# One batch's scores in two feed-forward banks, and two batches' small products issued form by form

## The chip, the cores and the metric

The kernel runs on one core of one Trainium2 chip. The metric is the device time of that core in microseconds (us). In what follows PE is the matrix engine (PEld its weight loads), DVE the vector engine, ACT the scalar engine, POOL the general one, and SP the engine whose queue issues nearly all transfers. PSUM is the memory into which PE writes its sums; it has eight banks.

## The reference, cut to what matters

The first half is a recurrent attention ("RetNet") over 768 tokens, 4 batches and 8 heads of 64 dimensions. Its output, with the heads of a token side by side (3072 tokens of 512 features), goes through a feed-forward network with a leaky rectifier.

```python
for t in range(S):
    state = gamma[None, :, None, None] * state + np.einsum('bhd,bhe->bhde', k[:, :, t], v[:, :, t])
    y[:, :, t] = scale * np.einsum('bhd,bhde->bhe', q[:, :, t], state)
...
h = x @ w_in
g = np.maximum(0.01 * h, h)
return (g @ w_out).astype(np.float32)
```

All of q, k, v are float32 here; the two weight matrices arrive as float64, so the kernel itself turns their 64-bit words into float32.

## The kernel before, in words

The recurrence is worked in chunks of 128 tokens (`C`), six chunks (`c` = 0 to 5) for each of four batches (`b` = 0 to 3). For one chunk of one batch the steps are these:

- `score` or `score_apart` (both through `scores_to`, line 182): 32 products of the chunk's keys and queries, with 64 rows and 64 columns of the PE array in use ("64*64" in the profile). `score` takes one tile of the pool tag `att` (two tiles of two banks each); `score_apart` takes two tiles of the tag `ff` (four tiles of one bank each, otherwise used by the feed-forward).
- `masked` (line 204) or, a half at a time, `masked_apart` (line 348): DVE multiplies the scores with the causal mask, out of PSUM into a tile `am`.
- `reads` (line 219): 16 products of the state with the queries, 64*64, the first to write the batch's tile `yp` (tag `att`). After them POOL does a tiny memset (line 224) that stands as an ordering mark: `first_values` of the same batch waits for it.
- `last_values` (line 255): 16 products of values and masked scores for the last 64 tokens of the chunk, in a form with all 128 rows and 64 columns ("128*64").
- `first_values` (line 244): 16 such products for the first 64 tokens, 64*64.
- `state` (line 270): 16 products of keys and values, 128*64, into other columns of the same tile `yp`.
- `taken`: DVE scales the tokens out of `yp` into the feed-forward's input `x` (line 300), adds the new sums to the state (line 309) and decays it (line 313). With the second of these the `yp` tile is given back.
- `decay_v` on ACT (line 154, eight instructions) scales the batch's values ahead of the products that read them.

The feed-forward is cut into four units of hidden columns, and each 2-by-2 product of blocks is done with seven block products instead of eight (`seven`, line 585; `hidden` and `output` are its two layers). Only unit 0 of chunk 0 is done with plain products (`direct`, line 607, tiles `d`), a step at a time (`next(steps)`). All of these use the whole array, "128*128".

The weights' float64 words are turned into float32 a piece at a time: `next_powers` puts three instructions on ACT (lines 497, 501, 502), `next_mantissas` three on DVE (lines 511, 516, 523) and then issues the load of a later piece on SP's queue.

The order of the work is written out by hand: each engine executes its instructions in the order in which the program's lines issue them, and engines wait for each other's results and for tiles to come free. The change lies in the straight-line part for chunk 1, between `scored_later(0)` and the second call of `products_together`. In this stage PE's order is: a step of `direct`; scores of batch 0; a step of `direct`; scores of batch 1; the products of batches 0 and 1 (`products_in_turn(0)`); a step of `direct`; scores of batches 2 and 3; the first block product of the next unit (`A_h`); the products of batches 2 and 3 (`products_together(2)`); the last step of `direct`; and the other block products. DVE's order is: mask of batch 0; a mantissa round; mask of batch 1; a mantissa round; `taken` for batches 0 and 1; masks of batches 2 and 3; and so on.

Of the kernel before, what the change touches and what calls it, by code (L numbers as in the profile page):

```python
# [23 lines left out]
def kernel(  # L24
# [133 lines left out]
    def two_banks(name):  # L158
        return psum.tile([128, 2, HP, C], FP32, tag="att", bufs=2, name=name)

    def score(c, b):

        ps = two_banks(f"ap_{c}_{b}").rearrange("p j a t -> p j (a t)")[:, :, 0:NS]
        scores[c, b] = ps.rearrange("p j (m n t) -> p j m n t", n=3, t=C // 2)
        scores_to(heads[c, b][0], [scores[c, b][:, j] for j in range(2)])
# [8 lines left out]
    def scores_to(x, ps):  # L174
        for m in range(HP // 2):
            for i in range(2):
                for late in range(2):
                    for j in range(2):
                        s, a = i ^ j, 2 * m + i
                        to = (ps[j][ts(1 - s, 64), m, 1 + s] if late else  # L180
                              ps[j][ts(s, 64), m, 0 : 2 + s : 1 + s])
                        nc.tensor.matmul(to, lhsT=x[ts(j, 64), 1, a, ts(late, 64)],  # L182
                                         rhs=x[ts(j, 64), 0, a, late * 64 :])
# [3 lines left out]
    def new_am(c, b):  # L187

        i = turn[0]
        turn[0] = (i + 1) % (3 if (c, b) >= (2, 2) else 2)  # L190
        if i < 2:
            return work.tile([128, 2, HP // 2, 3, C // 2], FP32, tag=f"am{i}", name=f"am_{c}_{b}")
        place = new_t(1, f"am_{c}_{b}").rearrange("p i k n -> p (i k n)")[:, 0 : 2 * NS]
        return place.rearrange("p (j m n t) -> p j m n t", j=2, n=3, t=C // 2)
# [7 lines left out]
    def masked(c, b):  # L202
        am = new_am(c, b)
        nc.vector.tensor_tensor(
            out=am.rearrange("p j m n t -> p j m (n t)"),
            in0=scores[c, b].rearrange("p j m n t -> p j m (n t)"),
            in1=mask.rearrange("p n t -> p (n t)").unsqueeze(1).unsqueeze(1)
                .to_broadcast([128, 2, HP // 2, 3 * C // 2]), op=ALU.mult)
        scores[c, b] = am
# [5 lines left out]
    def reads(c, b):  # L215
        x = heads[c, b][0]
        ps = sums_at[c, b] = two_banks(f"yp_{c}_{b}")
        for j, m, i, a in pairs:
            mm = nc.tensor.matmul(ps[ts(i, 64), j, m, :], lhsT=st[b][ts(j, 64), a, :],  # L219
                                  rhs=x[ts(j, 64), 0, a, :], start=(m == 0), stop=False,  # L220
                                  skip_group_check=True)


        reads_done[c, b] = nc.gpsimd.memset(between, 0.0).ins
        tc.add_manual_dep(reads_done[c, b], mm.ins.name, IN_ORDER, reason="rows of the array")
# [5 lines left out]
    def values(c, b):  # L231
        if c == 0:
            sums_at[c, b] = two_banks(f"yp_{c}_{b}")
        last_values(c, b)
        first_values(c, b)

    def first_values(c, b):

        y, am, ps = heads[c, b][1], scores[c, b], sums_at[c, b]
        for m in range(HP // 2):  # L240
            for i in range(2):
                for j in range(2):
                    s, a = i ^ j, 2 * m + i
                    mm = nc.tensor.matmul(ps[ts(i, 64), j, m, 0:64],  # L244
                                          lhsT=y[ts(s, 64), 1, 2 * a + j, :],
                                          rhs=am[ts(s, 64), j, m, 0], start=False, stop=True,
                                          skip_group_check=True)
                    if (c, b) in reads_done:
                        tc.add_manual_dep(mm.ins, reads_done.pop((c, b)).name, IN_ORDER,
                                          reason="rows of the array")  # L250

    def last_values(c, b):
        y, am, ps = heads[c, b][1], scores[c, b], sums_at[c, b]
        for j, m, i, a in pairs:
            nc.tensor.matmul(ps[ts(i, 64), j, m, 64:], lhsT=y[:, 1, 2 * a + j, :],  # L255
                             rhs=am[:, j, m, 1 + (i ^ j)], start=(c == 0 and m == 0), stop=True,
                             skip_group_check=True)

    def for_state(ps):
        return ps[:, 0, HP // 2 :, :].rearrange("p a (two d) -> p (a two) d", two=2)  # L260

    def state(c, b):
        y = heads[c, b][1]
        sp = for_state(sums_at[c, b])
        for a in range(HP) if c < NC - 1 else ():
            sums_of(sp, y, a)

    def sums_of(sp, y, a, start=False):
        for j in range(2):
            nc.tensor.matmul(sp[ts(j, 64), a, :], lhsT=y[:, 0, 2 * a + j, :],  # L270
                             rhs=y[:, 1, 2 * a + j, :], start=start, stop=True,
                             skip_group_check=True)
# [65 lines left out]
    def score_apart(c, b):  # L338

        banks = [psum.tile([128, HP * C], FP32, tag="ff", bufs=4, name=f"ap{j}_{c}_{b}")[:, 0:NS]  # L340
                 for j in range(2)]
        scores[c, b] = [ps.rearrange("p (m n t) -> p m n t", n=3, t=C // 2) for ps in banks]
        scores_to(heads[c, b][0], scores[c, b])

    def masked_apart(c, b, j):
        if j == 0:
            weights_of[c, b] = new_am(c, b)
        nc.vector.tensor_tensor(
            out=weights_of[c, b][:, j].rearrange("p m n t -> p m (n t)"),
            in0=scores[c, b][j].rearrange("p m n t -> p m (n t)"),  # L350
            in1=mask.rearrange("p n t -> p (n t)").unsqueeze(1)
                .to_broadcast([128, HP // 2, 3 * C // 2]), op=ALU.mult)
        if j == 1:
            scores[c, b] = weights_of.pop((c, b))
# [96 lines left out]
    def next_powers(scratch=None, between=None):  # L451
        n = done["powers"]
        done["powers"] += 1
        if n < N_PIECES and f64:
            powers(n, scratch, between)
        elif between is not None:
            between()
# [18 lines left out]
    def next_mantissas():  # L476
        begin_mantissas()
        end_mantissas()
# [389 lines left out]
        score(1, b)  # L868
        masked(1, b)

    def products_in_turn(b):
        for i in range(2):
            reads(1, b + i)
            values(1, b + i)
        for i in range(2):
            state(1, b + i)

    def products_together(b):
        for f in (reads, last_values, state, first_values):
            for i in range(2):  # L880
                f(1, b + i)

# [5 lines left out]
    scored_later(0)  # L890
    decay_v(1, 1, nc.scalar)
    next(steps)
    score(1, 1)
    next_powers()
    next_mantissas()
    masked(1, 1)
    next_powers()
    products_in_turn(0)
    next_mantissas()
    decay_v(1, 2, nc.scalar)  # L900
    next_powers()
# [8 lines left out]
    last_sum(0)  # L910
    next_mantissas()
    products_together(2)
    next_powers()
    run(steps, {})
# [144 lines left out]
```

## Time and profile before

| | us |
|---|---|
| median of 4 runs (lowest, highest) | 658.36 (657.75, 658.77) |
| profiled execution, its own time | 658.36 |
| its span, from the first to the last instruction | 656.5 |
| PE busy in the span | 651.6 |
| DVE busy | 362.4 |
| ACT busy | 176.1 |
| PE busy in the stretch from 30.58 to 34.81 (products of chunk 1, batches 0 and 1) | 4.23 of 4.23 |
| PE busy in the stretch from 40.16 to 43.83 (products of chunk 1, batches 2 and 3) | 3.67 of 3.67 |

The profiled execution took as long as the median, 658.36 us, of which 1.8 us lie outside the span. The granted clock of PE was 1.00 over the whole span. A line of a timeline gives the start, the duration up to the end of the last instruction merged into it, the engine, the line of the kernel, the operation, output and input by tile names, the part of the array in use, the shape and the number of instructions. Consecutive products overlap on PE, so the cost of a group of products is read from its start to the start of the next group, not from its own duration.

### The profile page before, as it was taken

What the parts mean: (1) busy time and instruction counts of PE and PEld (TensorE: products, weight loads), DVE (VectorE), ACT (ScalarE), POOL (GpSimd) and SP (SyncE); (2) the same over time, 40 slices, a digit from 0 to 9 for tenths busy, and PEclk for the clock granted to TensorE, in tenths of its full rate; (3) what the DMA queues carried; (4) which work ended last, traced back from release to release, by engine and by line L of the source; (5) the groups of instructions that cost most, each with busy time, mean ns of one, the idle gap of its engine ahead of it and who ended that gap; (6) DMA issues with size and microseconds to landing.
All of it is one profiled execution on the core that took longest, in us unless ns stands there. A gap on an engine that the chain in (4) does not pass through costs nothing.

```text
span 656.5 us, 11361 instructions
## 1 busy us (share of the span) xinstructions
PE 651.6 (99%) x4937; PEld 568.9 (87%) x4937; DVE 362.4 (55%) x589; ACT 176.1 (27%) x323; POOL 22.2 (3%) x45
## 2 busy tenths in 40 slices
PE   8999999999999999999999999999999999999998
PEld 5888888888888888888888889888888888888887
DVE  5789969889887674243436414526423344431342
ACT  5854465264261002102102211300220210221210
POOL 1000000000000020001001001001000100000000
PEclk9999999999999999999999999999999999999999
DMA  9921312323322650030022004004001001000001
GB/s 336 405 98 33 128 65 85 108 65 97 128 69 83 245 185 0 1 127 3 1 96 98 1 1 129 1 17 178 0 1 52 14 1 49 17 0 1 1 0 65
DMA packets 15906, 49.00 MB, mean 75 GB/s; under 512 B 1768, under 2 KB 2152, under 8 KB 15856
## 3 DMA queue, kind: packets, MB, share of 16 engines
q1 hardware_dynamic: 15696, 47.72, 20.9%
q8 instruction: 39, 0.64, 0.4%
q10 hardware_dynamic: 160, 0.55, 0.2%
q14 instruction: 11, 0.09, 0.0%
HBM read 41.97 MB, written 6.29 MB: 74 GB/s over the span
## 4 chain that ended last, share of the span: by engine, by line
PE 98%; DMA 1%; DVE 0%; issue 0%; DVEq 0%
PE B_o L585 13%; PE A_o L585 13%; PE C_o L585 13%; PE A_h L585 12%; PE B_h L585 12%; PE C_h L585 12%; PE D_o L585 6%; PE D_h L585 6%; PE ap L182 2%; PE d L607 2%; PE yp L255 2%; PE yp L219 1%; PE yp L244 1%; PE sp L270 1%; DMA t<-decay_dram 1%; PE yp L270 0%
## 5 line engine op out<-in xcount | busy, mean ns | idle before, releaser
L585 PE MATMUL A_h<-x,w 128*128 128x256 f32 x368 | 87.7, 381 | 0.0
L585 PEld LDWEIGHTS A_h<-x,w 128*128 128x128 f32 x368 | 69.3, 190 | 9.6
L585 PE MATMUL A_o<-g,w 128*128 128x256 f32 x288 | 68.1, 379 | 0.0
L527 DVE TENSOR_TENSOR m<-m,B_h 128x512 f32<-128x512 f32 x23 | 15.8, 687 | 92.9 <-PE B_h L585 92.9
L585 PEld LDWEIGHTS A_o<-g,w 128*128 128x128 f32 x288 | 54.6, 190 | 7.5
L620 ACT ACTIVATE g<-g 128x512 f32<-128x512 f32 x69 | 42.0, 630 | 66.3 <-DVE g L527 66.3
L625 ACT COPY m<-A_h 128x512 f32<-128x512 f32 x23 | 13.5, 586 | 170.5 <-PE A_h L585 150.2
L527 DVE TENSOR_TENSOR m<-m,B_o 128x512 f32<-128x512 f32 x16 | 11.0, 685 | 64.4 <-PE B_o L585 64.4
L585 PE MATMUL B_h<-t,w 128*128 128x256 f32 x184 | 43.6, 380 | 0.0
L585 PE MATMUL B_h<-x,w 128*128 128x256 f32 x184 | 43.5, 379 | 0.0
L585 PE MATMUL C_h<-t,w 128*128 128x256 f32 x184 | 43.5, 379 | 0.0
L585 PE MATMUL D_h<-t,w 128*128 128x256 f32 x184 | 43.5, 379 | 0.0
L585 PE MATMUL C_h<-x,w 128*128 128x256 f32 x184 | 43.5, 379 | 0.0
L585 PEld LDWEIGHTS B_h<-t,w 128*128 128x128 f32 x184 | 34.8, 190 | 5.1 <-DVE t L530 0.4
L585 PEld LDWEIGHTS B_h<-x,w 128*128 128x128 f32 x184 | 35.0, 190 | 4.8
L585 PEld LDWEIGHTS C_h<-t,w 128*128 128x128 f32 x184 | 35.0, 190 | 4.8
L585 PEld LDWEIGHTS D_h<-t,w 128*128 128x128 f32 x184 | 35.0, 190 | 4.8
L585 PEld LDWEIGHTS C_h<-x,w 128*128 128x128 f32 x184 | 35.0, 190 | 4.8
L585 PE MATMUL C_o<-gd,w 128*128 128x256 f32 (+1 forms) x148 | 34.2, 373 | 0.0
L585 PE MATMUL C_o<-g,w 128*128 128x256 f32 (+1 forms) x148 | 34.2, 373 | 0.0
L530 DVE TENSOR_TENSOR gd<-g,gd 128x512 f32<-128x512 f32 x48 | 33.2, 692 | 1.7
L585 PE MATMUL B_o<-gd,w 128*128 128x256 f32 x144 | 34.1, 380 | 0.0
(131 smaller groups left out, 986.4 us busy)
## 6 DMA issues: line engine op xcount, KB each, us to landing
raw<-in_weights_dram SPq DMA_DIRECT2D x31, 512.0 KB, 4.0
kv<-in_kv_dram SPq DMA_DIRECT2D x17, 512.0 KB, 5.3
out_dram<-o SPq DMA_DIRECT2D x23, 256.0 KB, 2.1
qk<-in_qk_dram SPq DMA_DIRECT2D x10, 512.0 KB, 4.8
o<-in_qk_dram SPq DMA_DIRECT2D x8, 512.0 KB, 4.7
in<-in_qk_dram SPq DMA_DIRECT2D x5, 512.0 KB, 8.3
in<-in_kv_dram SPq DMA_DIRECT2D x3, 512.0 KB, 7.8
kv<-in_kv_dram SPq DMA_DIRECT2D x4, 256.0 KB, 7.4
```

Source lines behind the costliest of these rows:

```text
L182: nc.tensor.matmul(to, lhsT=x[ts(j, 64), 1, a, ts(late, 64)], rhs=x[ts(j, 64), 0, a, late * 64 :])
L219: mm = nc.tensor.matmul(ps[ts(i, 64), j, m, :], lhsT=st[b][ts(j, 64), a, :], rhs=x[ts(j, 64), 0, a, :], start=(m == 0), stop=False, skip_g ...
L244: mm = nc.tensor.matmul(ps[ts(i, 64), j, m, 0:64], lhsT=y[ts(s, 64), 1, 2 * a + j, :], rhs=am[ts(s, 64), j, m, 0], start=False, stop=True, ...
L255: nc.tensor.matmul(ps[ts(i, 64), j, m, 64:], lhsT=y[:, 1, 2 * a + j, :], rhs=am[:, j, m, 1 + (i ^ j)], start=(c == 0 and m == 0), stop=Tru ...
L270: nc.tensor.matmul(sp[ts(j, 64), a, :], lhsT=y[:, 0, 2 * a + j, :], rhs=y[:, 1, 2 * a + j, :], start=start, stop=True, skip_group_check=True)
L527: nc.vector.tensor_tensor(out=out, in0=a, in1=b, op=ALU.add)
L530: nc.vector.tensor_tensor(out=out, in0=a, in1=b, op=ALU.subtract)
L585: nc.tensor.matmul(to, lhsT=block(w, sa)[:, k, ts(i, 128)], rhs=rhs[:, k, a:z], start=(first and (i == 0 or split) and n == 0 and k == 0), ...
L607: nc.tensor.matmul(banks[r][:, i, :], lhsT=block(2 * u, r + 2 * kh)[:, k, ts(i, 128)], rhs=x[:, 2 * kh + th, k, :], start=(step == 0 and i ...
L620: nc.scalar.activation(g[:, i], g[:, i], AF.Prelu, alpha=0.01)
L625: nc.scalar.copy(out=got["m1"], in_=ps)
```

## The change

Three things change, all in chunk 1.

- The scores of batch 1 go into two tiles of the feed-forward's tag `ff`, one bank each, rather than into one tile of the tag `att`. The products themselves are the same 32.
- DVE therefore masks them in two instructions of 128x384 (`masked_apart`), rather than in one of 128x768, at the same place in its order.
- The products of batches 0 and 1 are issued together: the reads of both; then the last values and the state of each; then the first values of both. Before, each batch had its reads, last values and first values in turn, and the states of both came behind. The function serves batches 2 and 3 as well, and there only the order inside the middle changes: last values and state of batch 2 and then of batch 3, rather than the last values of both and then the states of both.

```diff
-    def products_in_turn(b):
+    def products_together(b):
         for i in range(2):
             reads(1, b + i)
-            values(1, b + i)
-        for i in range(2):
+        for i in range(2):
+            last_values(1, b + i)
             state(1, b + i)
-
-    def products_together(b):
-        for f in (reads, last_values, state, first_values):
-            for i in range(2):
-                f(1, b + i)
+        for i in range(2):
+            first_values(1, b + i)
...
     scored_later(0)
     decay_v(1, 1, nc.scalar)
     next(steps)
-    score(1, 1)
+    score_apart(1, 1)
     next_powers()
     next_mantissas()
-    masked(1, 1)
+    for j in range(2):
+        masked_apart(1, 1, j)
     next_powers()
-    products_in_turn(0)
+    products_together(0)
     next_mantissas()
```

The two functions that are called in place of `score` and `masked` were there already, for later chunks:

```python
def score_apart(c, b):
    banks = [psum.tile([128, HP * C], FP32, tag="ff", bufs=4, name=f"ap{j}_{c}_{b}")[:, 0:NS]
             for j in range(2)]
    scores[c, b] = [ps.rearrange("p (m n t) -> p m n t", n=3, t=C // 2) for ps in banks]
    scores_to(heads[c, b][0], scores[c, b])

def masked_apart(c, b, j):
    if j == 0:
        weights_of[c, b] = new_am(c, b)
    nc.vector.tensor_tensor(
        out=weights_of[c, b][:, j].rearrange("p m n t -> p m (n t)"),
        in0=scores[c, b][j].rearrange("p m n t -> p m (n t)"),
        in1=mask.rearrange("p n t -> p (n t)").unsqueeze(1)
            .to_broadcast([128, HP // 2, 3 * C // 2]), op=ALU.mult)
    if j == 1:
        scores[c, b] = weights_of.pop((c, b))
```

## The prediction, made before the changed kernel ran

> **What bounds the kernel.** I read the page first: busy time by engine, and the chain that ended last.
>
> ```profile
> PE 651.6 (99%) x4937; PEld 568.9 (87%) x4937; DVE 362.4 (55%) x589; ACT 176.1 (27%) x323; POOL 22.2 (3%) x45
> PE 98%; DMA 1%; DVE 0%; issue 0%; DVEq 0%
> ```
>
> The reader is to see that PE is the bound from end to end: 98% of the chain is PE's own instructions. So what the change is worth is the time that it takes out of PE's sequence, less any wait that it puts in. Next I read PE's timeline over the two stretches that hold chunk 1's small products, and one place in a later chunk where 32 reads lie between products of their own form.
>
> ```profile
> 30.58 0.62 PE L219 MATMUL yp<-in,states 64*64 64x128 f32 x16
> 31.13 0.69 PE L255 MATMUL yp<-am,in 128*64 128x64 f32 x16
> 31.75 0.46 PE L244 MATMUL yp<-am,in 64*64 64x64 f32 x16
> 32.12 0.67 PE L219 MATMUL yp<-in,states 64*64 64x128 f32 x16
> 32.72 0.69 PE L255 MATMUL yp<-am,in 128*64 128x64 f32 x16
> 33.34 0.46 PE L244 MATMUL yp<-am,in 64*64 64x64 f32 x16
> 33.73 1.15 PE L270 MATMUL yp<-in 128*64 128x64 f32 x32
> 34.81 1.99 PE L607 MATMUL d<-x,w 128*128 128x256 f32 x8
> ...
> 40.16 0.67 PE L219 MATMUL yp<-in,states 64*64 64x128 f32 x16
> ...
> 41.19 0.69 PE L255 MATMUL yp<-am,in 128*64 128x64 f32 x16
> ...
> 43.49 0.41 PE L244 MATMUL yp<-am,kv 64*64 64x64 f32 x16
> 43.83 1.99 PE L607 MATMUL d<-x,w 128*128 128x256 f32 x8
> ...
> 233.55 1.06 PE L219 MATMUL yp<-o,states 64*64 64x128 f32 x32
> 234.43 0.85 PE L182 MATMUL ap<-qk 64*64 64x128 f32 x32
> ```
>
> Read the starts. The 128 products of batches 0 and 1 take 34.81 - 30.58 = 4.23 us; the 128 products of the same kinds of batches 2 and 3, which the kernel issues kind by kind already, take 43.83 - 40.16 = 3.67. The array's form (64*64, 128*64) changes six times from the first read to `direct` in the first stretch (reads, last, first and reads, last, first, state, `direct`), three times in the second. Last I read DVE over the same stretch, since it decides when scores are masked and when banks come free.
>
> ```profile
> 31.12 0.95 DVE L204 TENSOR_TENSOR am<-ap,mask 128x768 f32<-128x768 f32 x1
> 31.98 0.42 DVE L511 TENSOR_SCALAR w<-raw 128x512 uint32<-128x512 uint32 x1
> ...
> 34.46 0.69 DVE L300 TENSOR_TENSOR x<-yp,dec 128x512 f32<-128x512 f32 x1 [0.54 <-PE yp L270]
> ...
> 36.45 0.41 DVE L309 TENSOR_TENSOR states<-states,yp 128x256 f32<-128x256 f32 x1
> 36.90 0.43 DVE L313 TENSOR_TENSOR states<-states,dec 128x256 f32<-128x256 f32 x1
> 37.71 1.82 DVE L204 TENSOR_TENSOR am<-ap,mask 128x768 f32<-128x768 f32 x2 [0.39 <-PE ap L182]
> ...
> 233.80 1.02 DVE L348 TENSOR_TENSOR am<-ap,mask 128x384 f32<-128x384 f32 x2
> ```
>
> The first line hides a wait of PE. The mask of batch 1 ends at 31.12 + 0.95 = 32.07, and the reads of batch 1 begin at 32.12, since their `yp` tile is the one that held batch 0's or batch 1's scores, two `att` tiles being all there are. The first values before them began at 31.75, and such a group takes 0.28 when the same kind follows (row 43.49 against the start of its neighbour, 43.21, in the same timeline), so the reads could have begun at 32.03: about 0.09 us of PE time was lost to the mask.
>
> **The products of batches 0 and 1, on the path.** What will they take when grouped? The reads now follow scores of their own form. Sixteen reads followed by the same form cost half of 234.43 - 233.55, so 0.44; sixteen followed by the change to 128*64 cost 31.13 - 30.58 = 0.55; together 0.99. From the first of the last values to `direct` the row is that of batches 2 and 3: 43.83 - 41.19 = 2.64. Sum 3.63, against 4.23: **-0.60 us**. The other bound takes the whole stretch of batches 2 and 3 as it stands, 3.67, whose reads follow a 128*128 product and pay for it: -0.56. I take -0.60, since reads behind scores is what the new order has.
>
> **Last values and state interleaved, both pairs.** Both are 128*64, 16 products each. In the second stretch the groups of these two kinds start at 41.19, 41.71, 42.17, 42.64 and the next form at 43.21: 0.47 for each group inside the row, whether the neighbour is of the same kind or the other. Order inside one form is costed at 0. For batches 2 and 3 that is all that changes, so 0 there.
>
> **Scores of batch 1 in `ff` banks.** The same 32 products, 0. They now wait for two `ff` tiles. In the built program these are the banks of `direct`'s first pair of tiles, which ACT emptied by 26.1 (two instructions of 0.6 from 24.92), while PE reaches these scores at 29.87: covered by 3.8 us. The same two banks pass on to the A and B tiles of the next block products, exactly as before, 6 us after the masks; every later `ff` tile has the bank that it had. The `att` tiles alternate with the halves exchanged, at no cost that I can name.
>
> **The mask in two instructions, off the path.** The row 233.80 shows two of 128x384 in 1.02 us, so the pair ends 0.07 later than the one of 0.95, at 32.14, and DVE's next instruction starts some 0.09 later (second mask at 0.475, twice, against 31.98 - 31.12 = 0.86). Who waits? PE's last values of batch 1, which come behind reads (0.99), last values (0.52) and state (0.47) from 30.58: at 32.56. Cover 0.42 us; if it were gone, PE would wait for the difference, with `direct` queued behind. [...]
>
> **DVE's chain behind it.** Its mantissa round now ends at 33.92 + 0.09 = 34.01. The tokens of batch 0 (L300) waited in the trace for the last product into that `yp` tile, the state's, until 34.46. In the new order the last product into it is batch 0's first values: they start at 31.57 + 2.02 = 33.59 (43.21 - 41.19 = 2.02), 16 of them end at about 34.05. So L300 starts about 34.05, 0.41 earlier than before. Then batch 1's state is added by 36.86 - 0.41 = 36.45, which is what the scores of batch 3 need for their tile; PE reaches these at 37.45 - 0.60 = 36.85. **Cover 0.40 us**, the smallest on this path. The mask of batch 2 is ready to go at 37.33 - 0.41 = 36.92 and its scores end at 37.11: it moves by the full 0.60, as do `A_h`, the products of batches 2 and 3 and all that follows them.
>
> **POOL and SP.** POOL's two marks follow the reads; the second now comes at about 31.6 instead of 32.94, and the first values that wait for it start at 33.87. Nothing else is queued on POOL. SP's order is unchanged; the weight load behind the moved mantissa round is issued 0.09 later and its reader on ACT is at 51.52, some 14 us after landing (4.0 us each).
>
> **Sum.** -0.60 against the profiled execution's own 658.36 us, which is the median too: **657.76 us**, 0.09% less. About 0.2% (1.3 us) is what a measurement of this kernel tells from no change, so the forecast is "same" with a small real gain inside.
>
> **Rivals.**
> 1. *Slower: DVE becomes the wait.* If DVE is late by more than 0.40 us at batch 1's state, PE waits in front of batch 3's scores; from 0.40 + 0.60 = 1.00 the kernel is slower than before. A whole mantissa round between the wrong steps (1.94, from 31.98 to 33.92) would give 658.36 - 0.60 + 1.94 - 0.40 = 659.3. For it: DVE is 84% busy in this stretch (3.56 of 4.23), and the tokens of batch 0 now hang on the end of a group that comes later in the order. Against it: the instruction that DVE then waits for is earlier in time than before, and the order on DVE is otherwise the same.
> 2. *Absorbed.* PE comes 0.60 earlier to something that doesn't move, a transfer or a conversion: 658.36. For it: the transfers are busy here (0.96 of their time from 30.58 to 34.81). Against it: in the list of waits none of PE's after 27 us is a transfer, and the conversions of this stage run behind PE's own results.
> 3. *More.* PE stalls at 57.88 us for DVE's emptying of the B bank (DVE L527 ends at 57.82); the eight products before it take 57.88 - 56.02 = 1.86 and its own 59.71 - 57.88 = 1.83, where such a group takes 1.73 in the steady rows: 0.23 in all. If a changed order freed that, 658.36 - 0.60 - 0.23 = 657.53. Against: DVE is busy without a pause from 43.74 to there and starts on PE's last product, so it shifts as PE does, and the bank is the same.
>
> **From the numbers to the chances.** The forecast case has 0.82, absorbed 0.08, slower by DVE 0.06, more 0.04. Runs of the kernel lie 0.61 below to 0.41 above their median. That puts the likeliest case within 657.15 to 658.17, and with the absorbed case and a little of its scatter the range is 657.1 to 658.5. Beyond 1.3 us on the fast side there is no mechanism (0.03 for scatter); on the slow side a part of rival 1 (0.04); the rest is within 0.2%.
>
> **What would show it.** After: reads of both batches in one run from 30.58 for about 0.99 us; the stretch to `direct` 3.6 us; `direct` at 34.2; the masks as two rows ending at 32.14; L300 at 34.05; all later rows 0.6 earlier, the stall at 57.3 still there. Wrong would be: a gap before the last values of batch 1 (mask late), a gap before the scores of batch 3 (bank late), or the 0.6 vanishing at a later wait.

## The result and the profile after

The changed kernel takes 657.30 us (median of 41 runs) against 658.39 us for the kernel before (61 runs, taken beside them). The medians differ by 1.09 us. The ratio on record, which is that of the means (657.45 to 658.36), is 0.9986, with a 95% interval of 0.9982 to 0.9991: 0.14% faster, or 0.92 us (0.59 to 1.19). That is "same" on record and inside the 0.2% of the forecast, but the interval lies wholly below 1, so the gain is real. Two later comparisons of the same two kernels, with 11 runs of the changed kernel each, gave 0.9990 (0.9981 to 0.9999) and 0.9989 (0.9980 to 0.9997).

The profiled execution of the changed kernel took 657.73 us, 0.43 above the median; it has a pause of PE ahead of the stretch in question, of which more below. The page's first and fourth parts read as before:

```profile
PE 650.8 (99%) x4937; PEld 568.3 (87%) x4937; DVE 361.5 (55%) x590; ACT 176.1 (27%) x323; POOL 22.3 (3%) x45
PE 98%; DMA 1%; DVE 0%; issue 0%; DVEq 0%
```

PE's timeline over the two stretches of small products, changed kernel (columns as before: start, duration, engine, line, operation, tiles, form, shape, count):

```profile
31.06 1.05 PE L219 MATMUL yp<-in,states 64*64 64x128 f32 x32
32.04 0.69 PE L255 MATMUL yp<-am,in 128*64 128x64 f32 x16
32.56 0.64 PE L270 MATMUL yp<-in 128*64 128x64 f32 x16
33.02 0.64 PE L255 MATMUL yp<-am,in 128*64 128x64 f32 x16
33.49 0.64 PE L270 MATMUL yp<-in 128*64 128x64 f32 x16
34.06 0.69 PE L244 MATMUL yp<-am,in 64*64 64x64 f32 x32
34.68 1.99 PE L607 MATMUL d<-x,w 128*128 128x256 f32 x8
36.61 0.90 PE L182 MATMUL ap<-in 64*64 64x128 f32 x32
37.33 0.85 PE L182 MATMUL ap<-qk 64*64 64x128 f32 x32
...
40.03 0.67 PE L219 MATMUL yp<-in,states 64*64 64x128 f32 x16
...
43.71 1.99 PE L607 MATMUL d<-x,w 128*128 128x256 f32 x8
```

The first stretch lasts 34.68 - 31.06 = 3.62 us where it lasted 4.23. The second, whose middle was reordered too, lasts 3.67 as before (3.674 from the unrounded starts of both kernels). DVE over the same time:

```profile
31.59 1.01 DVE L348 TENSOR_TENSOR am<-ap,mask 128x384 f32<-128x384 f32 x2
...
34.59 0.69 DVE L300 TENSOR_TENSOR x<-yp,dec 128x512 f32<-128x512 f32 x1
...
36.59 0.41 DVE L309 TENSOR_TENSOR states<-states,yp 128x256 f32<-128x256 f32 x1
```

The two masks end at 32.60, before the last values of batch 1 at 33.02. Batch 1's state is added by 37.00, before the scores of batch 3 at 37.33. No new wait stands in the stretch.

The traces allow a sharper comparison than the times. From the unrounded starts of the products I take three figures of each trace: the first stretch (first read of batch 0 to the plain products), the second (first read of batch 2 to the plain products), and the time from the end of the first stretch to the start of the kernel's last product. "Pause" means, here and below, that PE stands still although nothing that the profile shows holds it up.

| kernel | stretch 1 | stretch 2 | behind stretch 1 | ratio to the kernel before |
|---|---|---|---|---|
| before, three traces | 4.22, 4.22, 4.92 | 3.67 | 618.69, 618.20, 618.19 | 1 |
| changed, three traces | 3.63, 3.62, 3.63 | 3.67 | 618.19, 618.20, 618.20 | 0.9986, 0.9990, 0.9989 |
| scores apart alone | 4.08 | 3.67 | 618.20 | 0.9998 |
| grouping alone | 4.78 | 3.67 | 618.19 | 1.0009 |
| order by kind | 3.78 | 3.67 | 618.18 | 0.9991 |
| second pair in turn | 3.63 | 4.13 | 618.42 | 0.9993 |
| one more on DVE | 3.63 | 3.67 | 618.55 | 0.9996 |
| three more on DVE | 3.63 | 3.67 | 619.85 | 1.0014 |
| last sum later | 3.63 | 3.67 | 617.96 | 0.9985 |
| ACT late | 3.72 | 3.67 | 618.39 | 0.9993 |

Behind the stretch, the kernel before and the changed one agree to 0.01 us, save the first trace of before, which has one pause there. So what the change does to a trace it does inside the stretch, and all that follows comes as much earlier.

### The profile page after: what moved, and what is told of

Same layout as the page of the kernel before. It is cut to its first block, busy times and chain, and to the rows that moved or that the text cites. A ratio compares the mean times of both kernels' runs of the same rounds, so it can differ in the third digit from the quotient of the medians.

```text
span 655.9 us, 11361 instructions
## 1 busy us (share of the span) xinstructions
PE 650.8 (99%) x4937; PEld 568.3 (87%) x4937; DVE 361.5 (55%) x590; ACT 176.1 (27%) x323; POOL 22.3 (3%) x45
## 4 chain that ended last, share of the span: by engine, by line
PE 98%; DMA 1%; DVE 0%; issue 0%; DVEq 0%
PE B_o L585 13%; PE A_o L585 13%; PE C_o L585 13%; PE A_h L585 12%; PE B_h L585 12%; PE C_h L585 12%; PE D_o L585 6%; PE D_h L585 6%; PE ap L182 3%; PE d L607 2%; PE yp L255 2%; PE yp L219 1%; PE yp L244 1%; PE sp L270 1%; DMA qk<-in_qk_dram 1%; PE yp L270 0%
```

## The experiments

**Which half of the change brings the gain: scores apart alone.** The kernel before, with only the scores and the mask of batch 1 changed.

```diff
-    score(1, 1)
+    score_apart(1, 1)
...
-    masked(1, 1)
+    for j in range(2):
+        masked_apart(1, 1, j)
```

> The kernel before with batch 1's scores in two feed-forward banks and the mask in two halves, products still batch by batch. By the prediction's steps the reads of batch 1 no longer wait for the mask: 0.09 us less, the stretch 4.14 instead of 4.23, or 4.09 if the restart of 0.05 inside the reads goes too; total -0.1. Rival (the feed-forward banks themselves bring a gain or a wait): more than 0.3 either way.

PE's timeline of this kernel:

```profile
30.30 0.62 PE L219 MATMUL yp<-in,states 64*64 64x128 f32 x16
...
31.46 0.46 PE L244 MATMUL yp<-am,in 64*64 64x64 f32 x16
31.74 0.62 PE L219 MATMUL yp<-in,states 64*64 64x128 f32 x16
...
34.38 1.99 PE L607 MATMUL d<-x,w 128*128 128x256 f32 x8
```

The stretch is 4.08. The reads of batch 1 follow the first values of batch 0 after 0.28, where it was 0.37 (32.12 - 31.75) in the kernel before: the mask's wait is gone, and with it 0.05 of restart inside the reads, which took 32.72 - 32.12 = 0.60 behind the stop and 32.29 - 31.74 = 0.55 here. The wait's price in the first trace was thus 0.14 us. The ratio, 0.9998 (0.9989 to 1.0007), cannot tell 0.1 from nothing; the trace can.

**Grouping alone.** The changed kernel with `score(1, 1)` and `masked(1, 1)` put back.

```diff
-    score_apart(1, 1)
+    score(1, 1)
...
-    for j in range(2):
-        masked_apart(1, 1, j)
+    masked(1, 1)
```

> The changed kernel with batch 1's scores back in one tile of the attention banks and one mask, products still grouped. The reads of batch 1 then need the tile that the mask reads last, so PE waits after the reads of batch 0 until about 32.1 where it could go on at 31.0: the stretch 3.63 + 1.1 = 4.7 us, total +0.5 against the kernel before. Rival (the banks don't matter, grouping alone brings it all): the stretch 3.6, total -0.6.

```profile
30.83 0.62 PE L219 MATMUL yp<-in,states 64*64 64x128 f32 x16
32.37 0.67 PE L219 MATMUL yp<-in,states 64*64 64x128 f32 x16 [0.92 <-DVE am L204]
...
35.60 1.99 PE L607 MATMUL d<-x,w 128*128 128x256 f32 x8
```

PE stands after batch 0's reads until the mask (DVE L204) frees the tile: a step of 1.54 in place of 0.44. The stretch is 4.78 and the kernel slower than before, ratio 1.0009 (1.0001 to 1.0018), as forecast. Grouping without the second pair of banks loses; the scores in feed-forward banks are what lets it gain.

**The price of a change of form.** With the mask's wait out of the way, batch by batch costs 4.08 and grouped 3.63: 0.45 us for three changes of the array's form, 0.15 each. In the starts of these two traces the price stands where the form changes: the first product after a change comes 0.15 or 0.20 after the one before it, and where a new kind begins in the same form 0.04 or 0.05. Does it hold elsewhere? The changed kernel with the products of batches 2 and 3 issued in turn:

```diff
+    def products_in_turn(b):
+        for i in range(2):
+            reads(1, b + i)
+            values(1, b + i)
+        for i in range(2):
+            state(1, b + i)
...
-    products_together(2)
+    products_in_turn(2)
```

> The changed kernel with the products of batches 2 and 3 issued batch by batch, as those of 0 and 1 were before: three changes of the array's form more, and no mask to wait for. The measured price of three changes without the mask's wait is 4.08 - 3.63 = 0.45 us (scores apart alone against the changed kernel). Expected: that second stretch 3.67 + 0.45 = 4.12 us, total +0.45 against the changed kernel, so about 0.15 to 0.2 below the kernel before. Rival (the price was due to the place, the mask and the scores before it): less than 0.2.

```profile
39.76 0.67 PE L219 MATMUL yp<-in,states 64*64 64x128 f32 x16
...
43.89 1.99 PE L607 MATMUL d<-x,w 128*128 128x256 f32 x8
```

The second stretch takes 4.13: the price is that of the form, not of the place. But the kernel's trace is only 618.42 - 618.19 = 0.23 longer behind the first stretch, not 0.46. Half was given back later, and DVE's timeline shows why. It starts on batch 2's tokens when the products into batch 2's tile are done. In this order that is 0.34 us before the plain products begin:

```profile
43.55 1.29 DVE L300 TENSOR_TENSOR x<-yp,dec 128x512 f32<-128x512 f32 x2 [1.55 <-PE yp L270]
```

In the changed kernel it starts 0.10 before them, at 43.61 against 43.71:

```profile
43.61 1.29 DVE L300 TENSOR_TENSOR x<-yp,dec 128x512 f32<-128x512 f32 x2 [1.32 <-PE yp L244]
```

From there DVE waits for nothing for 14 us, up to the emptying of a bank for which PE waits (at 57.8). A DVE that starts earlier by PE's clock removes that wait of 0.23, and PE's groups there step by 1.72 and 1.73 with the second pair in turn:

```profile
56.09 1.89 PE L585 MATMUL A_o<-g,w 128*128 128x256 f32 x8
57.81 1.89 PE L585 MATMUL B_o<-gd,w 128*128 128x256 f32 x8
59.54 0.81 PE L585 MATMUL C_o<-gd,w 128*128 128x256 f32 x3
```

**That wait, tried directly.** The changed kernel with one DVE subtraction moved behind the emptying:

```diff
-                2: [next_powers], 3: [lambda: add_sums(1)]})
+                2: [next_powers], 3: [lambda: add_sums(1, last=False)],
+                4: [lambda: last_sum(1)]})
```

> The changed kernel with one DVE subtraction (the last of the four weight sums of unit 1, 0.61 us from start to start) moved behind the emptying of the B bank, which PE waits for at 57.8. In every trace but that of the second pair in turn, DVE works without a pause from 43.6 to there and PE loses 0.13 before the group and 0.10 in its first product. Expected: the emptying ends at about 57.1, before PE needs it at 57.6, and the 0.23 go: 617.96 us from the plain products to the last product instead of 618.19, total 0.23 below the changed kernel. Rival (PE waits there for something else): 618.19.

PE's timeline, the changed kernel first (three groups of eight products), then this one:

```profile
55.90 1.89 PE L585 MATMUL A_o<-g,w 128*128 128x256 f32 x8
57.75 1.99 PE L585 MATMUL B_o<-gd,w 128*128 128x256 f32 x8
59.58 0.59 PE L585 MATMUL C_o<-gd,w 128*128 128x256 f32 x2
```

```profile
55.52 1.89 PE L585 MATMUL A_o<-g,w 128*128 128x256 f32 x8
57.25 1.89 PE L585 MATMUL B_o<-gd,w 128*128 128x256 f32 x8
58.98 1.24 PE L585 MATMUL C_o<-gd,w 128*128 128x256 f32 x5
```

Steps of 1.85 and 1.83 become 1.73 and 1.73, and the time behind the stretch falls to 617.96. This version measured 657.14 us, ratio 0.9985 (0.9976 to 0.9994) to the kernel before; beside the changed kernel of the same chip, 657.36, it is the faster of the two by 0.22, which the times alone would not prove and the trace does.

**The order inside a form.** The changed kernel with last values of both batches, then states of both:

```diff
-        for i in range(2):
-            last_values(1, b + i)
-            state(1, b + i)
-        for i in range(2):
-            first_values(1, b + i)
+        for f in (last_values, state, first_values):
+            for i in range(2):
+                f(1, b + i)
```

> The changed kernel with the middle ordered as last values of both, then states of both. Inside one form the order costs nothing, but the last values of batch 1 come 0.47 us earlier and then begin 0.05 us before the second half of the mask is done: the stretch 3.63 to 3.7 us, total within 0.1 of the changed kernel. Rival (alternating last values and states costs or saves something itself): the stretch differs by over 0.2.

```profile
30.34 1.05 PE L219 MATMUL yp<-in,states 64*64 64x128 f32 x32
31.32 1.31 PE L255 MATMUL yp<-am,in 128*64 128x64 f32 x32
32.46 1.10 PE L270 MATMUL yp<-in 128*64 128x64 f32 x32
...
34.12 1.99 PE L607 MATMUL d<-x,w 128*128 128x256 f32 x8
```

DVE's two masks in the same trace:

```profile
30.99 1.02 DVE L348 TENSOR_TENSOR am<-ap,mask 128x384 f32<-128x384 f32 x2
```

The stretch is 3.78, more than the 3.63 to 3.7 expected. The 32 last values take 1.14 where 0.99 is their price (0.52 + 0.47): PE waited 0.10 for the mask's second half, which ended at 32.01, and restarted 0.05 slower. But the masks of this trace were themselves 0.12 late, starting 0.65 after the first read instead of 0.53. By these figures masks on time would have cost nothing (an estimate, with 0.02 to spare). The changed kernel's third trace has the same lateness (0.66) and a stretch of 3.63. For the second pair the two orders take the same 3.67. So the order itself is free, and what the state products between the last values buy is cover for the mask, 0.47 us of it; that is why the same lateness cost 0.15 in one order and nothing in the other.

**How thin is DVE's cover.** One, then three subtractions of 128x512 more on DVE, between the masks and the mantissa round; three shown:

```diff
     products_together(0)
+    for _ in range(3):
+        minus(parts[1][2][:, 0], x[:, 0], x[:, 0])
     next_mantissas()
```

> The changed kernel with one more 128x512 subtraction on DVE, between the masks and the mantissa round; its result is overwritten before it is used. It delays DVE by about 0.65 us. By the trace batch 1's state is added 0.33 us before the scores of batch 3 need its bank, and DVE waited 0.1 for batch 0's products: expected cost on PE 0.65 - 0.1 - 0.33 = 0.2 us, as a pause before the scores of batch 3. Rival (DVE's cover is larger, the next wait is elsewhere): 0.

> The same with three such subtractions: 1.9 us later on DVE, expected cost 1.9 - 0.43 = 1.5 us, split over a pause before the scores of batch 2 and one before those of batch 3, total about 0.8 us above the kernel before. Rival: under 0.5.

PE's timeline with one more, then with three:

```profile
36.47 0.90 PE L182 MATMUL ap<-in 64*64 64x128 f32 x32
37.33 0.90 PE L182 MATMUL ap<-qk 64*64 64x128 f32 x32
```

```profile
34.22 1.99 PE L607 MATMUL d<-x,w 128*128 128x256 f32 x8
37.08 0.90 PE L182 MATMUL ap<-in 64*64 64x128 f32 x32 [0.87 <-issue]
38.47 0.90 PE L182 MATMUL ap<-qk 64*64 64x128 f32 x32 [0.49 <-PE ap L182]
```

With one, the scores of batch 3 come 0.86 after those of batch 2 instead of 0.72: 0.14 lost there, 0.2 expected. (Of the rest of its 618.55, 0.05 lies inside these scores and 0.16 is a pause in a later chunk, at 344.23.) With three, both scores wait, 0.93 (2.86 from the plain products instead of 1.93) and 0.67, and the time behind the stretch is 1.66 longer, 1.5 expected; ratio 1.0014 (1.0005 to 1.0023). The added work delays DVE's mantissa round by 0.60 and by 2.05 us, and PE loses 0.19 and 1.65 around these scores. The place and the cover are as forecast: DVE may be 0.4 us late and no more.

**Is the gain more than 0.60?** The three ratios say 0.7 to 0.9 us, a little above what the first traces show. I had two ideas: pauses of PE that happen to be absent, or something systematic. Both kernels were traced again.

> The changed kernel once more, for a second trace. The trace of before has a pause of PE of 0.48 us at 344.58 us, in the middle of a group of state products that waits for nothing; the changed kernel's trace has one of 0.61 us at 23.55 instead. Theory A (only the products count: 0.60 us, the rest is the scatter of such pauses): the pauses sit elsewhere again in this trace, and the stretch from the first read of batch 0 to the plain products is 3.63 us. Theory B (the change also takes away a pause that the kernel before nearly always has): the changed kernel is again about 1.0 us below the kernel before, and this trace has no pause, so that its own time is about 657.2.

> The kernel before once more, for a second trace. So far every trace has the same 618.19 us from the plain products after the stretch to the last product, within 0.01, save the first trace of before, which has 618.69 with its pause of 0.48 at 344.58. Theory A (pauses come and go): no pause at 344.58 here, 618.2 us. Theory B (the kernel before nearly always pauses there): 618.7 us again. The stretch is 4.22 either way.

> The changed kernel a third time, on the same chip as the next one. Theory A: 3.63 us for the stretch, 618.19 us behind it, and the comparison with the kernel before -0.6 us, with pauses of 0.3 to 0.6 us that come and go in both. Theory B (the change also saves some 0.3 us outside the stretch): -0.9.

> The kernel before a third time: 4.22 us for the stretch and 618.19 behind it, 618.5 to 618.7 if it has the pause at 344.58 again, or another inside.

The pause at 344.58 in the first trace of before didn't come again in its other two. The pause near 23.55 is in two of the changed kernel's three traces and in none of before's, though up to there both programs are the same: pauses come and go, and theory B in the form that I gave it (before nearly always pauses there) fell. But the third trace of before showed something else, in the stretch itself:

```profile
31.47 0.46 PE L244 MATMUL yp<-am,in 64*64 64x64 f32 x16
32.54 0.67 PE L219 MATMUL yp<-in,states 64*64 64x128 f32 x16 [0.61 <-DVE am L204]
...
35.23 1.13 PE L607 MATMUL d<-x,w 128*128 128x256 f32 x4
```

Here the reads of batch 1 waited 0.8 us for the mask. ACT and DVE of the same trace tell why the mask was late:

```profile
23.52 2.02 ACT L154 ACTIVATE in<-in,dec 128x64 f32<-128x64 f32 x8 [2.71 <-DMA in<-in_kv_dram]
...
29.67 0.43 DVE L511 TENSOR_SCALAR w<-raw 128x512 uint32<-128x512 uint32 x1 [0.90 <-ACT z L501]
...
31.54 0.95 DVE L204 TENSOR_TENSOR am<-ap,mask 128x768 f32<-128x768 f32 x1
```

A transfer of values landed late, so ACT began its scaling at 23.52 (23.00 in the first trace, with PE's reads at 30.58 there and 30.30 here); DVE's mantissa round (L511) waited 0.90 for ACT instead of 0.20; and the mask, which stands behind that round, started 1.23 after the first read instead of 0.53. (In the changed kernel's second trace ACT began as late, at 23.57, but there PE itself paused for 0.57, up to 23.64, so that by PE's clock the mask was on time.) The last run tests what the changed kernel makes of the same lateness, with an ACT copy more ahead of ACT's part of the conversion:

```diff
     score_apart(1, 1)
+    nc.scalar.copy(out=parts[1][2][:, 0], in_=x[:, 0])
     next_powers()
```

> The changed kernel with one more 128x512 copy on ACT (about 0.6 us), ahead of the conversion steps that DVE's mantissa round waits for; its result is overwritten before use. It makes batch 1's mask late, as a late transfer did by 0.70 us in the third trace of before, where the reads waited and the stretch grew from 4.22 to 4.92. Theory C (the mask is at times late, the kernel before pays for all of it, the changed kernel has 0.4 us of cover): the mask starts about 1.2 us after the first read instead of 0.53, the stretch grows by only 0.2, to 3.8 us, a pause before the third of batch 1's last values, and the total is 0.2 to 0.3 above the changed kernel. Rival (the changed kernel pays as much): the stretch 4.2 to 4.3.

```profile
31.63 1.01 DVE L348 TENSOR_TENSOR am<-ap,mask 128x384 f32<-128x384 f32 x2
```

```profile
30.57 1.05 PE L219 MATMUL yp<-in,states 64*64 64x128 f32 x32
...
32.53 0.73 PE L255 MATMUL yp<-am,in 128*64 128x64 f32 x16
33.09 0.64 PE L270 MATMUL yp<-in 128*64 128x64 f32 x16
34.28 1.99 PE L607 MATMUL d<-x,w 128*128 128x256 f32 x8
```

The mask started 1.06 after the first read, 0.53 later than in an undisturbed trace, and the stretch grew by 0.09, to 3.72: the last values of batch 1 take 0.56 to the next group instead of 0.47, the wait being before the third pair of them, where the second half of the mask is first needed. The kernel before paid 0.70 for 0.70 of lateness; the changed one 0.09 for 0.53, so by an estimate from these two figures it would pay 0.26 for 0.70. That is a second gain, which a trace without the lateness doesn't contain. (Behind the stretch this run is 0.2 longer, 0.03 of it before the scores of batch 3 and most of the rest in a pause at 343.81.)

How much of the measured 0.7 to 0.9 us it makes up on average stays open: the mask was late by over 0.1 in one of three traces of before, by 0.12 or 0.13 in two of ten others, and the pauses scatter by as much as the difference.

## Why the prediction was right, and what it missed

*The sum.* The range (657.1 to 658.5) and the class ("same") held; 657.76 was forecast and 657.30 measured. The forecast gain of 0.60 lies only just inside the first comparison's interval (0.59 to 1.19), so the total is not as well explained as the main term. The main term, -0.60 for the products of batches 0 and 1, is what the traces show: 4.22 became 3.63, of which "scores apart alone" puts 0.14 down to the mask's wait, and the rest is the form's. The way of getting it, from rows of groups that already stood in the wanted order with the wanted neighbours, was good to 0.01. Its upper bound, the second stretch as it stands (-0.56), was 0.04 off: the first sixteen of those reads, which follow a 128*128 product, took 0.49 (40.03 to 40.52 in the changed kernel), and sixteen behind scores 0.44.

*The mis-sized term.* "About 0.09 us of PE time was lost to the mask" is the step that came out too small. In the first trace it was 0.14 (0.09 before the reads and 0.05 of restart inside them, in the sum but not in the sentence). And it is not a constant: it was 0.84 in another execution of the same kernel. I read the wait in one trace, saw it just begin, and did not ask what happens when the mask is late by a transfer. The measured gain lies 0.1 to 0.3 above the forecast, on the side to which this points.

*The mask in two instructions.* The pair took 1.01 in the changed kernel, as the older row had it, and DVE's next instruction followed 0.93 after the first mask began, 0.06 later than 0.87 and not 0.09. It cost nothing. The row, not the durations added up, is what DVE's clock sees: two halves of 0.55 against one whole of 0.95 are 0.15 more by durations, but the halves started 0.47 apart, and by starts the pair costs the 0.06.

*The middle order, POOL, the banks: costed at nothing.* For the second pair the stretch was 3.67 either way. For the first pair the order is what gives the mask its cover, as "order by kind" showed; the forecast had the cover (0.42, with the state's 0.47 in its sum) and did not say that without the state between them it would be gone. POOL's second mark came at 32.26, well before the first values at 34.06. The banks brought no wait of their own: "scores apart alone" gained the mask's 0.14 and nothing else.

*Rival 1, DVE becomes the wait.* The place (the scores of batch 3) was right and so was the size: 0.40 of cover forecast, 37.33 - 37.00 = 0.33 and 0.1 of slack before L300 in the trace, and the two doses of DVE work fit. It needed a delay that the change doesn't bring.

*Rival 2, absorbed.* Nothing behind the stretch took the gain back: 618.19 to 618.20 us in all traces of the two kernels without a pause there.

*Rival 3, more.* The stall at 57.8 stayed, since DVE moves with PE, as argued; moving one instruction removed it, as shown.

## What to carry to other kernels

Price a regrouping of small products by the starts of groups that already have the neighbours they will have, not by durations or counts; here a change of the array's form cost 0.15 us each. When one trace shows a wait that has only just begun, look for what can make its releaser late: a change that moves the waiting work behind half a microsecond of other work can be worth more in the times than in that trace (here 0.70 us of lateness cost 0.70 before, and 0.53 cost 0.09 after). And where two engines run nearly level, half of a gain or loss on one may come back at the next place where it waits for the other (here 0.23 of 0.46 us).

## What the runs showed of the hardware

In some of these traces PE paused for 0.2 to 0.6 us in the middle of a group of products that, by the profile, had nothing to wait for. In the changed kernel's first trace:

```profile
22.80 0.32 PE L244 MATMUL yp<-am,in 64*64 64x64 f32 x2
23.55 0.45 PE L244 MATMUL yp<-am,in 64*64 64x64 f32 x14 [0.42 <-issue]
```

Five of the fourteen traces have a pause before this same product, the third of the group. In all fourteen that product starts 1.33 to 1.58 us after a 16 KB packet of the instruction queue (q8 of the page) has landed (22.18 here; between 21.25 and 21.76 in the nine traces without the pause, between 21.89 and 22.18 in the five with it). In the five the packet landed 0.62 to 0.86 us before the group's first product, in the nine 1.20 to 1.44. Three traces (the first of before, "one more on DVE", "ACT late") pause at one other product, near 344 us, and there too the packet had landed latest by PE's clock: 0.39 to 0.72 before its group's first product, against 0.80 to 1.17 in the other eleven.

That queue moved 39 packets and 0.64 MB in the whole run, and PE's records of one trace, weight loads included, number 9942. By an estimate from these figures (0.64 MB over 9942 records) it comes to 64 bytes a record and to 256 records in a 16 KB packet. The two products at which PE paused lie 5119 to 5122 records apart in all traces, and 20 x 256 is 5120. That PE waited there for its own instructions is a guess from these coincidences: no run changed the loading, and it is not shown.
